# Sum of the values made once per head and added by VectorE, in the last two pairs of each later batch

## The chip, the cores and the metric

The kernel runs on one core of a Trainium2 chip. The metric is the device time of one execution in microseconds (us). TensorE does the matrix products and transposes into PSUM, VectorE, ScalarE and GpSimd work element by element, and SyncE mostly issues the transfers. VectorE and ScalarE read PSUM, and so each matmul's result has to be picked up by one of them.

## The reference

Attention over hash buckets, followed by a channel mix. B = 4 batches, H = 8 heads, S = 768 rows, D = 64.

```python
q_bucket = sum(((q @ proj) > 0) * 2**arange(6)); k_bucket likewise
scores = where(q_bucket[i] == k_bucket[j], q k^T / 8, -1e9)
attn = exp(scores - max); attn = attn / (attn.sum(-1) + 1e-9)
x = (attn @ v), heads side by side           # [B, S, 512]
xk, xr = mixes of x and x shifted by one row with mu_k, mu_r
out = sigmoid(xr @ w_r) * (max(xk @ w_k, 0)**2 @ w_v)
```

A row of q whose bucket no key shares gets the mean of all rows of v: all its scores are equal. The kernel must give that too.

## The kernel before, in words

Two heads make a pair n; there are 16 pairs, 0 to 15, four to a batch (`NPB` = 4). A head's keys are cut into six blocks of 128 (`NC_` = 6). The main loop has 192 slots, G = 12 n + s: slot s of pair n does head j = s // 6, key block jc = s % 6. In each slot `score` makes the block's scores for all 768 queries (L487, two matmuls of 384 columns), and ScalarE takes the exponential (L494) into a tile `pt`. Two slots later (`LAG` = 2) `pv` multiplies it with the values: six matmuls L515, one per query block, 65 columns each (64 of v and a column of ones, which gives the row's sum), all accumulated in one PSUM bank `oo` of 128x390 floats. Between these, in an order that is written out by hand and fixed when the program is made, stand the matmuls of the channel mix of the batch before (`ffn`, L584: `kp`, `rp`, `vp`), the preparation of pair n + 2 (`prepare`: VectorE's stream transposes L384, GpSimd's casts L389, the hash bits L446 with their signs L399), and the outputs of pair n - 1 (`turn_out` in slot 3).

The mean of the values enters as a very small weight on every key, EPS = 2^-60. GpSimd's `values` sums v over the six key blocks into `vs` (128x65). In `pv`, at a head's first block, one matmul L506 with the constant matrix `epsm` (128x128, all EPS) and `vs` repeated six times writes EPS times the sum of all values into the six query blocks of `oo`; the L515 matmuls add to it.

At a head's last block VectorE takes the reciprocal of the row sums (`rc`, L526) and writes the scaled head to `ob` (L527). The first head ends in slot 7 of its pair, the second in slot 1 of the next. In slot 3 of the next pair `turn_out` turns `ob` with six transposes L544 into a bank `ot`, VectorE copies it into `xt` (L545, L549), and the mix of x and its shifted rows follows on VectorE (L555, L569, L572). Behind L527 in VectorE's queue there can also stand `os` (L642, the product that ends an output block of the channel mix) and `k` (L621, a square).

Four PSUM banks serve `oo`, `ot`, the bits and the channel mix. `take` gives the one that has been free longest, and `give` puts it back once its last reader has been issued; the next writer waits for that reader. The scores have two buffers of two banks each of their own.

Of the kernel before, what the change touches and what calls it, by code (L numbers as in the profile page):

```python
# [9 lines left out]
FP32 = mybir.dt.float32  # L10
BF16 = mybir.dt.bfloat16
INT32 = mybir.dt.int32
AF = mybir.ActivationFunctionType
ALU = mybir.AluOpType
AX = mybir.AxisListType

P = 128
# [7 lines left out]
EPS = 2.0 ** -60  # L25
# [11 lines left out]
def kernel(  # L37
# [13 lines left out]
    nc = tc.nc  # L51
    B, H, S, D = q.shape
# [3 lines left out]
    NC_ = S // P  # L56
    HALF = S // 2
    NDC = DM // P
    NFC = DF // P
    NPB = H // 2  # L60
    NPAIRS = B * NPB
    NTE = 4
# [7 lines left out]
    epsm = consts.tile([P, P], BF16, name="epsm")  # L70
# [97 lines left out]
    def fast():  # L168
        with ExitStack() as fx:
            pool = lambda nm, bufs, **kw: fx.enter_context(  # L170
                tc.tile_pool(name=nm, bufs=bufs, **kw)
            )
# [7 lines left out]
            ptp = pool("pt", 6)  # L180
            obp = pool("ob", 2)
            rcp = pool("rc", 4)
            xtp = pool("xt", 2)
            aug = pool("aug", 1)
            dfp = pool("df", 2)
# [11 lines left out]
            def take(shape, dt, name):  # L197
                which = idle_banks.pop(0)
                return which, bkp.tile(shape, dt, name=name, tag=f"bk{which}")

            def give(which):
                idle_banks.append(which)
# [3 lines left out]
            NSET = 3  # L206
# [4 lines left out]
            augs, vas, vss = [], [], []  # L211
# [16 lines left out]
            nats, blks, vfs, pts, obs, xts, t32s, oos, held = ({} for _ in range(9))  # L228
# [251 lines left out]
            def score(n, j, jc):  # L480
# [18 lines left out]
                    scale=SCALE / 2.0 if (n, j) == TWICE else SCALE,  # L499
                )  # L500

            def pv(n, j, jc):
                if jc == 0:
                    taken, oos[n, j] = take([P, NC_, D + 1], FP32, f"oo{n}_{j}")
                    held[n, j] = taken
                    nc.tensor.matmul(  # L506
                        oos[n, j],
                        epsm,
                        vss[n % NSET][j][:, None, :].to_broadcast([P, NC_, D + 1]),
                        start=True,  # L510
                        stop=False,
                    )
                oo = oos[n, j]
                for ic in range(NC_):
                    nc.tensor.matmul(  # L515
                        oo[:, ic, :],
                        pts[n, j, jc][:, ic * P : (ic + 1) * P],
                        vas[n % NSET][j][:, jc, :],
                        start=False,
                        stop=(jc == NC_ - 1 and ic == NC_ - 1),  # L520
                    )
                if jc == NC_ - 1:
                    if j == 0:
                        obs[n] = obp.tile([P, NC_, P], BF16, name=f"ob{n}", tag="ob")
                    rc = rcp.tile([P, NC_], FP32, name=f"rc{n}_{j}", tag="rc")
                    nc.vector.reciprocal(rc, oo[:, :, D])  # L526
                    nc.vector.scalar_tensor_tensor(  # L527
                        out=obs[n][:, :, j * D : (j + 1) * D],
                        in0=oo[:, :, 0:D],
                        scalar=ROOT_HALF,  # L530
                        in1=rc.to_broadcast([P, NC_, D]),
                        op0=ALU.mult,
                        op1=ALU.mult,
                    )
                    give(held.pop((n, j)))

            def turn_out(n):
                b, t = divmod(n, NPB)
                xt = xtp.tile([P, P + S], BF16, name=f"xt{n}", tag="xt")
                held[n], ot = take([P, S], BF16, f"ot{n}")  # L540

                for i in range(NC_):
                    c = 2 * (i % 3) + i // 3 if n < NTE else i
                    nc.tensor.transpose(ot[:, c * P : (c + 1) * P], obs[n][:, i, :], ident16)  # L544
                nc.vector.tensor_copy(xt[:, P : P + S], ot)  # L545
                xts[b, t] = xt, ot

                nc.vector.memset(xt[:, 0:1], 0.0)
                nc.vector.tensor_copy(xt[:, 1:P], ot[:, S - P : S - 1])  # L549


            mx = {}
# [337 lines left out]
            def outputs(n, s):  # L890
                if n < 1:
                    return
                if s == 3:
                    turn_out(n - 1)
                if s == 4:
                    pieces.extend(mix((n - 1) // NPB, (n - 1) % NPB))
                if pieces and s >= 4:
                    pieces.pop(0)()
# [58 lines left out]
            for G in range(nslots + LAG):  # L957
                clock[0] = G
                n, s = divmod(G, 12)
# [13 lines left out]
                if old and not first:  # L973
                    pv(*old)
# [11 lines left out]
                if old and first:  # L986
                    pv(*old)
# [12 lines left out]
            ffn(2 * rate)  # L1000
            step()
            turn_out(NPAIRS - 1)
            for x, op in enumerate(mix(B - 1, NPB - 1)):
                if x < 3:
# [194 lines left out]
    with tc.manual_schedule():  # L1199
        fast()  # L1200
# [33 lines left out]
```

## Time and profile before

| | |
|---|---|
| median of three runs | 250.59 us (250.33 to 250.74) |
| profiled execution, its own time | 250.4 us |
| its span, first to last instruction | 248.5 us |
| TensorE busy | 240.3 us, 97% of the span |
| ScalarE busy | 208.6 us, 84% |
| VectorE busy | 167.7 us, 67% |
| GpSimd busy | 113.5 us, 46% |
| granted TensorE clock, mean | 0.996 |

The profile is of one execution. PE is TensorE, PEld its weight loads (they overlap the matmuls), DVE VectorE, ACT ScalarE, POOL GpSimd; SPq, ACTq are queues that issue transfers. L12 is line 12 of the kernel before. A group's row gives the tiles written and read, the partitions and elements, how often, the busy time, and the mean duration. The "idle before" of a row is time in which its engine stood still ahead of it, with what ended the wait. A few per cent of the matmul records are missing from the trace, which shows as a step that is one matmul too long. Some of the numbers are steps from one start to the next or the distance from one instruction's end to another's start, read from the timeline.

### The profile page before, as it was taken

The page shows a single profiled execution, that of the slowest core. Times are in us where ns is not written, and L with a number is a line of the kernel's source. Part 1 is how long each engine was busy: PE and PEld are TensorE (multiplying, and loading weights), DVE is VectorE, ACT ScalarE, POOL GpSimd, SP SyncE. Part 2 cuts the span into 40 slices and gives each one's busy share as a digit, 9 for nine tenths or more (in the row PEclk, how much of TensorE's full clock was granted, in tenths as well). Part 3 has the DMA queues.
Part 4 walks back from the last instruction along what each step waited for, and adds up shares of the span by engine and source line. Part 5 has one row for each costly group of instructions (what it writes and reads, how often), then busy time and mean ns, then how long its engine had stood idle before and what let it go on. Part 6 is the DMA issues. An engine that isn't in the chain of part 4 may idle for free.

```text
span 248.5 us, 6652 instructions
## 1 busy us (share of the span) xinstructions
PE 240.3 (97%) x2422; PEld 145.9 (59%) x2444; DVE 167.7 (67%) x389; ACT 208.6 (84%) x344; POOL 113.5 (46%) x214
## 2 busy tenths in 40 slices
PE   7999999999999999999999999999999999999993
PEld 4576666565656655565656556565666565555442
DVE  2887887887887738575787838476696627399421
ACT  4899999999999979789999979789999999639510
POOL 5989877697546370815537280815528000000000
PEclk9999999999999999999999999999999999999998
DMA  6989879396999384948729485955920111120132
GB/s 203 377 188 241 191 181 201 111 184 172 193 218 198 111 208 120 257 87 223 164 78 226 113 187 148 254 123 164 181 69 6 49 42 45 48 79 3 48 125 92
DMA packets 28231, 36.71 MB, mean 148 GB/s; under 512 B 3216, under 2 KB 25376, under 8 KB 28192
## 3 DMA queue, kind: packets, MB, share of 16 engines
q1 hardware_dynamic: 25744, 33.21, 50.9%
q0 software_dynamic: 2160, 2.62, 6.8%
q8 instruction: 21, 0.34, 0.7%
q10 hardware_dynamic: 288, 0.39, 0.5%
q14 instruction: 18, 0.15, 0.2%
HBM read 31.99 MB, written 6.29 MB: 154 GB/s over the span
## 4 chain that ended last, share of the span: by engine, by line
PE 85%; ACT 8%; DMA 4%; issue 1%; SPq 1%; DVE 0%; ACTq 0%
PE sc L487 23%; PE vp L584 16%; PE kp L584 16%; PE oo L515 12%; PE rp L584 8%; ACT pt L494 7%; PE bb L446 3%; DMA qk<-in_q_dram 2%; PE tp L327 2%; PE oo L506 2%; PE ot L544 2%; DMA aq<-sg 2%; PE bb L419 1%; ACT kr L615 0%; ACT sq L310 0%
## 5 line engine op out<-in xcount | busy, mean ns | idle before, releaser
L494 ACT ACTIVATE pt<-sc 128x768 bf16<-128x768 f32 x192 | 151.2, 814 | 16.3 <-PE sc L487 13.6
L487 PE MATMUL sc<-aq,ak 70*128 70x384 bf16 (+1 forms) x384 | 93.8, 325 | 1.4 <-ACT pt L494 0.5
L515 PEld LDWEIGHTS <-pt 128*128 128x128 bf16 x1152 | 60.6, 97 | 26.4
L515 PE MATMUL oo<-va,pt 128*128 128x65 bf16 x1152 | 66.3, 193 | 0.0
L584 PE MATMUL kp<-xk,wk_sb 128*128 128x384 bf16 x256 | 52.8, 326 | 0.2 <-ACT kr L615 0.2
L584 PE MATMUL vp<-wv_sb,k 128*128 128x512 bf16 (+1 forms) x184 | 50.4, 369 | 0.6
L487 PEld LDWEIGHTS <-ak 70*128 70x128 bf16 (+1 forms) x384 | 34.3, 97 | 26.9 <-issue 4.6
L389 POOL TENSOR_SCALAR aq<-t 64x768 bf16<-64x768 f32 x24 | 19.9, 828 | 61.1 <-DVE t L384 39.8
L621 DVE TENSOR_TENSOR k<-kr 128x384 bf16<-128x384 bf16 x64 | 28.5, 455 | 11.7 <-ACT kr L615 11.2
L642 DVE SCALAR_TENSOR_TENSOR os<-th,vp 128x512 f32<-128x512 bf16 (+1 forms) x25 | 16.6, 663 | 19.5 <-PE vp L584 13.0
L584 PEld LDWEIGHTS <-wk_sb 128*128 128x128 bf16 x256 | 21.6, 97 | 13.6 <-issue 3.8
L615 ACT ACTIVATE kr<-kp 128x384 bf16<-128x384 f32 x50 | 25.0, 499 | 4.4 <-PE kp L584 4.4
L584 PE MATMUL rp<-wr_sb,xr 128*128 128x512 bf16 x90 | 26.8, 379 | 0.3
L584 PEld LDWEIGHTS <-k 128*128 128x128 bf16 x200 | 16.8, 97 | 10.8 <-issue 1.3
L632 ACT ACTIVATE th<-rp 128x512 bf16<-128x512 f32 x24 | 14.2, 593 | 10.0 <-PE rp L584 8.0
L389 POOL TENSOR_SCALAR ak<-t 64x768 bf16<-64x768 f32 x24 | 20.2, 840 | 5.0 <-DVE t L384 1.7
L384 DVE STREAM_TRANSPOSE t<-bl 128x768 f32<-128x768 f32 x24 | 22.3, 956 | 0.0
L545 DVE COPY xt<-ot 128x768 bf16<-128x768 bf16 x16 | 8.9, 558 | 19.3 <-PE ot L544 19.3
L310 ACT ACTIVATE sq<-bl 128x768 bf16<-128x768 f32 x24 | 20.2, 841 | 0.0
L475 POOL TENSOR_TENSOR s<-vf 128x192 f32<-128x192 f32 x32 | 19.9, 622 | 0.0
L527 DVE SCALAR_TENSOR_TENSOR ob<-oo,rc 128x384 bf16<-128x384 f32 x32 | 17.8, 557 | 1.1
L473 POOL CAST va<-vf 128x384 bf16<-128x384 f32 x32 | 16.9, 527 | 3.3 <-DMA vf<-in_v_dram 2.5
(76 smaller groups left out, 220.1 us busy)
## 6 DMA issues: line engine op xcount, KB each, us to landing
bl<-in_q_dram SPq DMA_DIRECT2D x48, 176.0 KB
bl<-in_k_dram SPq DMA_DIRECT2D x48, 176.0 KB
vf<-in_v_dram SPq DMA_DIRECT2D x15, 384.0 KB
out_dram<-os SPq DMA_DIRECT2D x18, 256.0 KB
out_dram<-os SPq DMA_DIRECT2D x12, 128.0 KB
qk<-in_q_dram SPq DMA_DIRECT2D x3, 384.0 KB
qk<-in_k_dram SPq DMA_DIRECT2D x3, 384.0 KB
wk_sb<-in_moe_w_k_dram POOLq DMA_DIRECT2D x2, 512.0 KB, 6.8
```

Source lines behind the costliest of these rows:

```text
L310: nc.scalar.activation(junk, src, AF.Square, accum_out=acc)
L384: nc.vector.transpose(t32(n)[:, i].rearrange("p h (c f x) -> p (h c) f x", c=3, f=4), src)
L389: eng.tensor_scalar(out=augs[n % NSET]["qk"[i], j][ROWS[j], :], in0=t32(n)[ROWS[j], i].rearrange("p h y -> p (h y)"), scalar1=(1.0, ALPHA)[i],
L473: nc.gpsimd.tensor_copy(to, of)
L475: nc.gpsimd.tensor_add(s3, vf[:, 0 : 3 * D], vf[:, 3 * D : 6 * D])
L487: nc.tensor.matmul(sc[:, sp, 0:HALF], au["k", j][kr, jc * P : (jc + 1) * P], au["q", j][kr, sp * HALF : (sp + 1) * HALF], start=True, stop ...
L494: nc.scalar.activation(pt.rearrange("p (s q) -> p s q", s=2), sc[:, :, 0:HALF], AF.Exp, bias=EXP_BIAS, scale=SCALE / 2.0 if (n, j) == TWIC ...
L515: nc.tensor.matmul(oo[:, ic, :], pts[n, j, jc][:, ic * P : (ic + 1) * P], vas[n % NSET][j][:, jc, :], start=False, stop=(jc == NC_ - 1 and ...
L527: nc.vector.scalar_tensor_tensor(out=obs[n][:, :, j * D : (j + 1) * D], in0=oo[:, :, 0:D], scalar=ROOT_HALF, in1=rc.to_broadcast([P, NC_, D]),
L584: nc.tensor.matmul(box["t"], lhs(), rhs(), start=(i == 0), stop=(i == len(mms) - 1))
L615: nc.scalar.activation(kr, kp, AF.Relu)
L621: 1, lambda: nc.vector.tensor_tensor(out=k2, in0=kr, in1=kr, op=ALU.mult)
```

## The change

In pairs 6, 7, 10, 11, 14 and 15 (`late`: the last two pairs of batches 1, 2 and 3) the L506 matmul at a head's start is left out, and the head's first L515 matmul opens the accumulation. Instead, in `turn_out` of the pair before, two matmuls with `epsm` make EPS times the sum of all values once for each head, 64 columns each, in the part of the bank `ot` that the transposes leave free (768 bf16 columns are 384 floats, and 128 of the bank's 512 remain). VectorE copies them to two constant tiles `vb`, whose 65th column GpSimd sets once at the start. At such a head's end VectorE adds `vb`, repeated six times, to `oo` and writes the sum to a tile `su` in SBUF. The reciprocal and the scaled write read `su`, and the bank of `oo` is given back after the add.

```diff
+            vbs = [sup.tile([P, D + 1], FP32, name=f"vb{j}") for j in range(2)]
+            for vb in vbs:
+                nc.gpsimd.memset(vb[:, D : D + 1], float(NC_ * P) * EPS)
+
+            def late(n):
+                return n >= NTE and n % NPB in (2, 3)
...
             def pv(n, j, jc):
                 if jc == 0:
...
-                    nc.tensor.matmul(
-                        oos[n, j],
-                        epsm,
-                        vss[n % NSET][j][:, None, :].to_broadcast([P, NC_, D + 1]),
-                        start=True,
-                        stop=False,
-                    )
+                    if not late(n):
+                        nc.tensor.matmul(
...
-                        start=False,
+                        start=(late(n) and jc == 0 and ic == 0),
                         stop=(jc == NC_ - 1 and ic == NC_ - 1),
                     )
                 if jc == NC_ - 1:
...
+                    if late(n):
+                        su = sup.tile([P, NC_, D + 1], FP32, name=f"su{n}_{j}", tag="su")
+                        nc.vector.tensor_tensor(
+                            su, oo, vbs[j][:, None, :].to_broadcast([P, NC_, D + 1]), op=ALU.add
+                        )
+                        give(held.pop((n, j)))
+                        oo = su
                     rc = rcp.tile([P, NC_], FP32, name=f"rc{n}_{j}", tag="rc")
                     nc.vector.reciprocal(rc, oo[:, :, D])
...
-                    give(held.pop((n, j)))
+                    if not late(n):
+                        give(held.pop((n, j)))

             def turn_out(n):
...
-                held[n], ot = take([P, S], BF16, f"ot{n}")
-
+                held[n], bank = take([P, 512], FP32, f"ot{n}")
+                ot = bank[:, 0:HALF].bitcast(BF16)
+                if n + 1 < NPAIRS and late(n + 1):
+                    for j in range(2):
+                        nc.tensor.matmul(
+                            bank[:, HALF + j * D : HALF + (j + 1) * D],
+                            epsm,
+                            vss[(n + 1) % NSET][j][:, 0:D],
+                            start=True,
+                            stop=True,
+                        )
                 for i in range(NC_):
...
                 nc.vector.tensor_copy(xt[:, 1:P], ot[:, S - P : S - 1])
+                if n + 1 < NPAIRS and late(n + 1):
+                    for j in range(2):
+                        nc.vector.tensor_copy(
+                            vbs[j][:, 0:D], bank[:, HALF + j * D : HALF + (j + 1) * D]
+                        )
```

`sup` is a new SBUF pool with one buffer per tile. The bank that each `take` returns, and the order of all other instructions on each engine, are the same in both programs.

More of the change, by code (lines that the diff above doesn't have):

```diff
@@ L182, in fast @@
             rcp = pool("rc", 4)
+            sup = pool("su", 1)
             xtp = pool("xt", 2)
@@ L505, in pv @@
                     held[n, j] = taken
-                    nc.tensor.matmul(
-                        oos[n, j],
-                        epsm,
-                        vss[n % NSET][j][:, None, :].to_broadcast([P, NC_, D + 1]),
-                        start=True,
-                        stop=False,
-                    )
+                    if not late(n):
+                        nc.tensor.matmul(
+                            oos[n, j],
+                            epsm,
+                            vss[n % NSET][j][:, None, :].to_broadcast([P, NC_, D + 1]),
+                            start=True,
+                            stop=False,
+                        )
                 oo = oos[n, j]
@@ L539, in turn_out @@
                 xt = xtp.tile([P, P + S], BF16, name=f"xt{n}", tag="xt")
-                held[n], ot = take([P, S], BF16, f"ot{n}")
+                held[n], bank = take([P, 512], FP32, f"ot{n}")
[4 more added lines that the diff above has]
+                            bank[:, HALF + j * D : HALF + (j + 1) * D],
+                            epsm,
+                            vss[(n + 1) % NSET][j][:, 0:D],
+                            start=True,
+                            stop=True,
+                        )
                 for i in range(NC_):
@@ L549, in turn_out @@
                 nc.vector.tensor_copy(xt[:, 1:P], ot[:, S - P : S - 1])
+                if n + 1 < NPAIRS and late(n + 1):
+                    for j in range(2):
+                        nc.vector.tensor_copy(
+                            vbs[j][:, 0:D], bank[:, HALF + j * D : HALF + (j + 1) * D]
+                        )
             mx = {}
```

## The prediction

> **What bounds the kernel now.** I read the page first (busy shares, the 40 slices, the chain that ended last), because they say which engine's time is the kernel's time.
>
> ```profile
> PE 240.3 (97%) x2422; PEld 145.9 (59%) x2444; DVE 167.7 (67%) x389; ACT 208.6 (84%) x344; POOL 113.5 (46%) x214
> PE   7999999999999999999999999999999999999993
> PE 85%; ACT 8%; DMA 4%; issue 1%; SPq 1%; DVE 0%; ACTq 0%
> ```
>
> TensorE is busy in every slice after the first, and 85% of the chain is its work; VectorE, which is to get the new work, has no share of the chain. A busy share can hide stalls, so next come the waits between 74 and 216 us, the stretch that holds pairs 6 to 15 and so every place that the change touches.
>
> ```profile
> DVE xt L545 <- PE ot L544: 14.8, 10, 2.3
> ...
> DVE rc L526 <- PE oo L515: 10.2, 6, 3.6
> ...
> PEld L584 <- issue: 5.0, 8, 0.6
> ...
> PE sc L487 <- issue: 0.2, 1, 0.2
> ```
>
> The columns are total us, times, and the longest. VectorE waits for TensorE (25.0 us in these two rows); no row has TensorE waiting for VectorE. The gaps of up to 0.6 us are weight loads, which run ahead of the matmuls: at 102.23 a load stands 0.62 us after the one before it, while the eight fp32 matmuls L446 are still at work. The table of stages says how much room the others have there.
>
> ```profile
> 130.70:159.10 28.40, 28.14 (x284) 16.39 (x287) 18.42 (x39) 25.26 (x41) 14.56 (x26) 1.00 0.73 182
> ...
> 187.30:216.20 28.90, 28.63 (x287) 17.40 (x291) 15.49 (x36) 25.39 (x41) 4.61 (x10) 1.00 0.11 40
> ```
>
> After the stretch and its length come PE, PEld, DVE, ACT, POOL, then the granted clock (1.00). In pairs 10 and 11 (first line) TensorE is busy for 28.14 of 28.40 us, VectorE for 18.42: 10 us of VectorE are free per two pairs. In pairs 14 and 15 it is 13.4 us. ScalarE is the next fullest, with some 3 us free. So TensorE's instruction stream is the time here, and what is taken out of it comes back one to one as long as nothing it needs arrives later.
>
> **What is taken out.** The change touches heads of pairs 6, 7, 10, 11, 14 and 15, so 12 heads. Each loses one L506 matmul of 390 columns. Its cost is not its duration (331 ns) but the step from its start to the next start, since matmuls overlap:
>
> ```profile
> 140.23 0.38 PE L584 MATMUL vp<-wv_sb,k 128*128 128x512 bf16 x1
> 140.44 0.33 PE L506 MATMUL oo<-vs,epsm 128*128 128x390 bf16 x1
> 140.61 0.34 PE L515 MATMUL oo<-va,pt 128*128 128x65 bf16 x6
> 140.79 0.49 PE L487 MATMUL sc<-aq,ak 128*128 128x384 bf16 x2
> ```
>
> L506 starts at 140.44 and the next matmul at 140.61: 0.17 us. The same step stands at the other late heads I read. 12 x 0.17 = 2.04 us removed. The wait for a free bank and for `vs` moves from L506 to the first L515; there is no time in it, since no such wait shows now.
>
> **What is added on TensorE.** Two matmuls of 64 columns with a weight load each, ahead of the transposes of `turn_out`, in six pairs: 12 in all. The nearest row is L515, 65 columns with a load each: six of them take the step from 140.61 to 140.79, 0.030 us each. 12 x 0.030 = 0.36 us. The far bound is that none of them overlaps: an L515 matmul's whole duration, 193 ns, 12 x 0.193 = 2.3 us, which would eat the gain. I take 0.030, because these loads use the same stream and the loads of L515 stay hidden in it 1152 times. The Trainium skill (TensorE: Matmul & The Clock Gate, Back-to-back issue gap) speaks against the change here: it gives about 81 ns per matmul in a stream of weight loads and 128-column matmuls. By it the 12 would be 0.97 us, and the net gain on TensorE 1.07 instead of 1.68. The trace does not agree with it: the six 128-column transposes L544 with a load each take 0.50 us, the last lasting 0.219, so 56 ns apart.
>
> Net on TensorE: 2.04 - 0.36 = 1.68 us.
>
> **What is added on VectorE.** Per head an add of 128x390 floats from PSUM. The row nearest is L527, the scaled write of 128x384 from PSUM, 557 ns; L642 with 512 columns takes 684, so 1.0 ns per column and 563 for 390. A dependent VectorE instruction starts 0.03 to 0.04 us after the one before it ends (`rc` to `ob`), so the chain at a head's end grows by 0.60 us. `rc` and `ob` then read SBUF. Bounds for `ob`: 398 ns (L345, 384 floats SBUF to SBUF, one tensor) and today's 557; I take 557. Per pair two copies of 64 columns from PSUM: about 0.22 us each (L549, 127 bf16 columns from PSUM, takes 220; by L527 less 320 columns it is 237). Sum: 12 x (0.60 + 0.22) = 9.8 us over six pairs, 1.6 us a pair, against the 5 to 6.7 us free per pair. It does not make VectorE the bound; what counts is where it is late.
>
> One thing is not in that sum. `ob` now has both inputs in SBUF, and such instructions stretch when GpSimd works:
>
> ```profile
> L527 DVE SCALAR_TENSOR_TENSOR ob<-oo,rc x32: 556/557/558, 15.8 to 215.3; 128x384 bf16<-128x384 f32 x32
> L621 DVE TENSOR_TENSOR k<-kr x64: 346/358/1006, 55.4 to 229.4; 128x384 bf16<-128x384 bf16 x64
> ```
>
> The numbers are minimum, median, maximum. L527, one input in PSUM, never varies, though it too runs beside GpSimd. L621, both inputs in SBUF, goes from 346 to 1006 ns, and the long ones lie beside GpSimd work, as the 864 ns at 130.35. So `ob` can lose up to 0.65 us at the second heads of pairs 6, 7, 10 and 11, where GpSimd prepares `values` at that time (0.3 to 0.6 us per instruction); at first heads GpSimd is idle until the stream transposes that follow, and in pairs 14 and 15 it has almost nothing left. The Trainium skill (SBUF — State Buffer, SBUF: two separate sides) says the same of a VectorE instruction with two SBUF inputs against a GpSimd one that reads SBUF: one blocks for the whole of the other. The trace agrees, with the 1006 against 346.
>
> **Who waits for that.** (a) The transposes L544 need `ob`. Pair 10's second head: `ob` ends at 147.58 and the weight load for its transposes starts at 148.87, 1.29 us later; for 6, 7, 11 and 14 the distance is 1.51, 1.28, 1.29, 1.28. TensorE gets there up to 0.11 sooner where the next head also loses its L506. 0.60 is covered, 0.60 + 0.5 just so. (b) Pair 15's has no such cover:
>
> ```profile
> 215.11 0.20 DVE L526 RECIPROCAL rc<-oo 128x6 f32<-128x6 f32 x1 [3.64 <-PE oo L515]
> 215.34 0.56 DVE L527 SCALAR_TENSOR_TENSOR ob<-oo,rc 128x384 bf16<-128x384 f32 x1
> ...
> 216.21 0.54 PEld L544 LDWEIGHTS <-ob 128*128 128x128 bf16 x6
> ```
>
> `ob` ends at 215.90, the load starts at 216.21. With the add, `ob` ends at 215.11 + 0.56 + 0.04 + 0.19 + 0.04 + 0.56 = 216.50, plus 0.04 to be seen: TensorE stands still for 0.33 us (0.15 if `ob` takes 398). (c) Banks that VectorE frees: behind the add in its queue is `os` L642, which frees the bank of a `vp`; I paired each bank's release with its next first write in the timeline, and the nearest cases that stand behind an added instruction are 0.92 to 1.24 us apart (vp's bank freed at 151.32, written again at 152.24). The copies (0.44) or the add (0.60) use part of it. (d) The stream transposes L384 behind the first head's add feed the bits L446: 0.55 us of cover in pair 7 (100.90 to 101.45), 1.3 to 2.0 in 6, 10 and 11. In pair 7 VectorE idles 0.44 before `os` at 94.02 and 0.59 before `os` at 99.32, waiting for TensorE; the copies and the add fall into these. Nothing lost. (e) ScalarE in pairs 14 and 15 runs without a gap for some stretches (from 193.84 to 204.1), and the scores there follow the exponential that frees their buffer by 0.12 us at the least. I take 0.05 us lost. (f) GpSimd's two one-column memsets at the start (0.1 us) stand before the first cast, whose result is needed half a microsecond later.
>
> Sum: 1.68 - 0.33 - 0.05 = 1.30 us less. The profiled execution took 250.4 (span 248.5 and 1.9 around it) and would take 249.1; the median of the runs is 250.59, 0.19 above it, so 249.3.
>
> **Rivals.** *The gain is mostly eaten on TensorE or by ScalarE* (0.14): a 64-column matmul is too short to hide the load behind it, so that the 12 cost 0.056 each, as the transposes do, instead of 0.03 (0.3 us more), and ScalarE, with 3 us free per two pairs, holds the scores back by 0.05 in each of the six late pairs (0.3 more): 249.9. For it speaks the 0.12 us of (e), against it the even steps of L515. The 81 ns that the Trainium skill gives (TensorE: Matmul & The Clock Gate, Back-to-back issue gap) would give the same: 1.07 - 0.38 = 0.69 less, 249.9. *VectorE's chain becomes what TensorE waits for, and it ends slower* (0.12): the six second heads have about 1.17 to 1.4 us of cover after the sooner arrival. An add of a form not seen in this trace (a float operand broadcast over six blocks) could take 1.0 us instead of 0.56; with 0.65 lost to GpSimd the delay is 1.69, so 0.52 us of standstill at four heads, none in pair 14, and 0.77 in pair 15: 2.85 lost against 1.68, time 251.8. It decides from a delay of about 1.45 us on. Against it: L527, also with a broadcast second input, takes 557 each time. *The change does nothing of the kind* is out: in the built programs' lists of instructions the 12 matmuls are gone and the 12 short ones are there, with the rest of TensorE's order kept.
>
> **How the numbers follow.** The forecast has 0.74; its own range is 248.9 (no tail loss) to 249.7. Some 0.2%, 0.5 us, is what a measurement can tell from no change. Faster by more: 0.74 and half of the first rival, 0.81; within: 0.07; slower: 0.12. The range for 8 in 10 runs from 248.8 to 250.2, which takes in the first rival and the bounds of the short matmuls up to about 0.1 each.
>
> **What would show it.** L506 count 20, not 32; steps of 0.03 at the 64-column matmuls; the add at about 560 ns; `ob` at 557 and longer in pairs 7, 8, 11 and 12 at their starts; a TensorE gap of 0.2 to 0.35 us before the last six transposes and no new wait of TensorE for VectorE elsewhere. The prediction is wrong if such waits stand before L544 in several pairs, or if the pairs with late heads don't shorten by 0.28 us each.

## The result and the profile after

The changed kernel takes 249.88 us (median of 19 runs, 248.74 to 250.75), the kernel before 250.80 in 19 runs made beside them. The ratio is 0.9949, 95% interval 0.9932 to 0.9967: 0.5% faster, 1.3 us of 250.8 (0.8 to 1.7). The two medians alone are 0.92 us apart. Forecast were 1.30 us less and a time of 249.3.

The page after, answering to the three lines shown of before. Line numbers are those of the kernel that a profile is of: the scores, L487 before, are L488 after.

```profile
PE 240.4 (97%) x2444; PEld 145.7 (59%) x2444; DVE 177.2 (71%) x413; ACT 208.4 (84%) x344; POOL 114.7 (46%) x216
...
PE   8899999999999999999999999999999999999992
...
PE 85%; ACT 7%; DMA 4%; issue 1%; SPq 1%; DVE 0%; ACTq 0%
```

VectorE has 9.5 us more to do (167.7 to 177.2) and still no share of the chain. TensorE's busy sum is no smaller, and that says little: a union of recorded spans depends on which records are missing (22 more matmul records here, of the same number of instructions).

The profiled execution took 250.22 us with a span of 248.1, only 0.4 less than before's 248.5, because the first scores start 0.69 us later (8.76 against 8.07) and the last write ends 0.34 us longer after the last `os`. Both belong to transfers. The transposes ahead of the first scores, in TensorE's timeline, before and then after (start, us, what, and in brackets the idle time ahead):

```profile
7.71 0.52 PE L327 MATMUL tp<-ident,qk 128*128 128x128 f32 x3 [0.19 <-DMA qk<-in_q_dram]
```

```profile
8.41 0.52 PE L328 MATMUL tp<-ident,qk 128*128 128x128 f32 x3 [0.88 <-DMA qk<-in_q_dram]
```

They wait for a piece of q to land, which came 0.7 us later in this execution. So I compare a **stretch**: from the first score matmul to the end of the last `os`. It is 236.82 us before and 235.34 after, 1.48 less. The distances between the first scores of neighbouring pairs split it (us, from the timelines; the last column is from pair 15's first score to the last `os`):

| | 5 | 6 | 7 | 8 | 9 | 10 | 11 | 12 | 13 | 14 | 15 and tail |
|---|---|---|---|---|---|---|---|---|---|---|---|
| before | 14.16 | 14.20 | 14.14 | 14.10 | 14.17 | 14.20 | 14.14 | 14.10 | 14.17 | 13.31 | 44.23 |
| after | 14.16 | 13.93 | 13.87 | 14.10 | 14.17 | 13.93 | 13.87 | 14.10 | 14.17 | 13.04 | 44.11 |

Each pair with late heads is 0.27 shorter, the others are the same to 0.01, and pair 15 gives back part of its 0.27. From pair 5 to the last `os` it is 184.93 before and 183.44 after, 1.49 less. The step where L506 (now L516) stood, in the timeline of TensorE:

```profile
134.94 0.22 PE L563 MATMUL ot<-vs,epsm 128*128 128x64 bf16 x2
134.99 0.50 PE L572 MATMUL ot<-ident,ob 128*128 128x128 bf16 x6
...
140.28 0.38 PE L617 MATMUL vp<-wv_sb,k 128*128 128x512 bf16 x1
140.49 0.34 PE L525 MATMUL oo<-va,pt 128*128 128x65 bf16 x6
140.67 0.49 PE L488 MATMUL sc<-aq,ak 128*128 128x384 bf16 x2
```

`oo` follows the `vp` matmul by 0.21, as L506 did before; the 0.17 is gone. The two short ones take 0.055 together. The waits between 74 and 216 us:

```profile
DVE su L538 <- PE oo L525: 10.0, 6, 3.5
DVE xt L573 <- PE ot L572: 9.6, 10, 1.3
...
PEld L617 <- issue: 5.6, 9, 0.6
...
PEld L572 <- DVE ob L545: 0.5, 1, 0.5
PEld L525 <- ACT pt L495: 0.2, 1, 0.2
```

VectorE's wait for the transposes fell from 14.8 to 9.6: the longer chains at the second heads used that idle time. TensorE waits for VectorE once. VectorE's new groups:

```profile
L545 DVE SCALAR_TENSOR_TENSOR ob<-su,rc 128x384 bf16<-128x384 f32 x12 | 7.7, 644 | 0.4
...
L538 DVE TENSOR_TENSOR su<-oo,vb 128x390 f32<-128x390 f32 x12 | 6.7, 562 | 10.0 <-PE oo L525 10.0
...
L580 DVE COPY vb<-ot 128x64 f32<-128x64 f32 x12 | 2.1, 215 | 0.0
```

The add takes 562 ns, a copy 215, `ob` from `su` 644 on average.

### The profile page after: what moved, and what is told of

Its sections match the earlier page's. It is cut to its first block, busy times and chain, and to the rows that moved or that the text cites. A ratio compares the mean times of both kernels' runs of the same rounds, so it can differ in the third digit from the quotient of the medians.

```text
span 248.1 us, 6709 instructions
## 1 busy us (share of the span) xinstructions
PE 240.4 (97%) x2444; PEld 145.7 (59%) x2444; DVE 177.2 (71%) x413; ACT 208.4 (84%) x344; POOL 114.7 (46%) x216
## 4 chain that ended last, share of the span: by engine, by line
PE 85%; ACT 7%; DMA 4%; issue 1%; SPq 1%; DVE 0%; ACTq 0%
PE sc L488 23%; PE vp L617 17%; PE kp L617 16%; PE oo L525 12%; PE rp L617 8%; ACT pt L495 6%; PE bb L447 3%; DMA qk<-in_q_dram 2%; PE tp L328 2%; PE ot L572 2%; DMA aq<-sg 2%; PE bb L420 1%; PE oo L516 1%; ACT sq L311 0%; SPq L253 0%
## 5 line engine op out<-in xcount | busy, mean ns | idle before, releaser
L488 PE MATMUL sc<-aq,ak 70*128 70x384 bf16 (+1 forms) x384 | 93.8, 325 | 1.1 <-ACT pt L495 0.5
L617 PE MATMUL vp<-wv_sb,k 128*128 128x512 bf16 (+1 forms) x200 | 54.4, 370 | 0.0
L488 PEld LDWEIGHTS <-ak 70*128 70x128 bf16 (+1 forms) x384 | 34.4, 98 | 26.9 <-issue 4.6
L654 DVE TENSOR_TENSOR k<-kr 128x384 bf16<-128x384 bf16 x64 | 29.1, 465 | 11.6 <-ACT kr L648 11.2
L617 PE MATMUL rp<-wr_sb,xr 128*128 128x512 bf16 x96 | 27.7, 379 | 0.0
L476 POOL TENSOR_TENSOR s<-vf 128x192 f32<-128x192 f32 x32 | 21.2, 664 | 0.0
L538 DVE TENSOR_TENSOR su<-oo,vb 128x390 f32<-128x390 f32 x12 | 6.7, 562 | 10.0 <-PE oo L525 10.0
```

What stands on the lines that cost most here:

```text
L476: nc.gpsimd.tensor_add(s3, vf[:, 0 : 3 * D], vf[:, 3 * D : 6 * D])
L488: nc.tensor.matmul(sc[:, sp, 0:HALF], au["k", j][kr, jc * P : (jc + 1) * P], au["q", j][kr, sp * HALF : (sp + 1) * HALF], start=True, stop ...
L617: nc.tensor.matmul(box["t"], lhs(), rhs(), start=(i == 0), stop=(i == len(mms) - 1))
L654: 1, lambda: nc.vector.tensor_tensor(out=k2, in0=kr, in1=kr, op=ALU.mult)
```

## The experiments

The pair distances of one profile, and with them the stretch, carry most verdicts, because the runs' times scatter by a few tenths of a per cent. In the profiles the pairs from 5 on repeat to 0.01 us where the program is the same; the early ones do not (pairs 0 and 1 together took 20.75 to 21.50 over all runs), so a stretch can be off by some 0.7, and the verdicts are read from the pairs.

**What L506 costs.** The kernel before, with L506 twice at the 12 heads:

```diff
+                    for x in range(2 if n >= NTE and n % NPB in (2, 3) else 1):
-                    nc.tensor.matmul(
+                        nc.tensor.matmul(
                             oos[n, j], epsm, vss[...],
                             start=True,
-                            stop=False,
+                            stop=(x == 0 and n >= NTE and n % NPB in (2, 3)),
                         )
```

> The kernel before, with L506 issued twice at the 12 late heads. Theory (one L506 costs its step, 0.17 us, not its duration, 0.331): 12 x 0.17 = 2.04 us more than before, stretch 238.85. Rival (its duration counts): 4.0 us more; rival (it lies beside other work): no change.

Pairs 6, 7, 10, 11 and 14 became 14.54, 14.48, 14.54, 14.48 and 13.65 long: 0.34 each, 0.17 per matmul, and the last piece 0.35. That is 2.05 in all; the stretch (239.18) is 2.36 longer, and the rest lies in pairs 0 and 1. Time 253.18 against 251.05, ratio 1.0092 (1.0061 to 1.0123). The step is the price.

**What the short matmuls cost.** Four times each:

```diff
-                    for j in range(2):
+                    for j in (0, 1) * 4:
                         nc.tensor.matmul(
                             bank[:, HALF + j * D : HALF + (j + 1) * D], epsm, ...
```

> The changed kernel with the two 64-column matmuls in turn_out made four times each: 36 more. Theory (0.028 us each, as their step in the trace of the changed kernel): 1.0 us more, stretch 236.35. Rival (some 0.08 us each, load and matmul together): 2.9 us more, stretch 238.2. The step in the trace, and the stretch, tell which.

```profile
134.84 0.40 PE L563 MATMUL ot<-vs,epsm 128*128 128x64 bf16 x8
135.07 0.50 PE L572 MATMUL ot<-ident,ob 128*128 128x128 bf16 x6
```

Eight take 0.23: 0.029 each. The pairs are 0.17 to 0.18 longer than in the changed kernel (14.10, 14.04, 14.11, 14.05, 13.21), 0.028 to 0.03 for each of the six more; the stretch is 236.29. The Trainium skill (TensorE: Matmul & The Clock Gate, Back-to-back issue gap) gives about 81 ns per load and matmul of 128 columns; neither these (29 ns) nor the 128-column transposes (56 ns apart) come to it, and the measurement decides. Time 250.65 against 251.13, ratio 0.9975 (0.9938 to 1.0012).

**Whether VectorE's work counts.** The add made twice:

```diff
                     if late(n):
...
+                        for _ in range(2):
-                        nc.vector.tensor_tensor(
+                            nc.vector.tensor_tensor(
```

> The changed kernel with the add at each of the 12 late heads made twice: 12 x 0.60 = 7.2 us more for VectorE, TensorE's stream the same. Theory (VectorE's work costs only where it outruns the cover before the transposes): ob ended 0.42 to 0.77 us ahead of the load in pairs 6, 7, 10, 11 and 14, so the doubled add uses up the cover and loses at most 0.2 in each; pair 15 loses 0.6 more; together 0.6 to 1.5, stretch 235.9 to 236.8. Rival (VectorE's busy time counts as such): 7.2 us more, stretch 242.

The stretch is 236.59, 1.25 more, and pairs 5 to 15 give 1.19 of it, where VectorE got 12 x 0.60 = 7.2 us more. The waits between 74 and 218 us name the largest part:

```profile
PEld L573 <- DVE ob L546: 1.1, 1, 1.1
...
PE ot L573 <- DVE ob L546: 0.6, 1, 0.6
```

That is pair 15 (44.71 instead of 44.11). Pairs 7 and 11 are 0.15 and 0.17 longer, because the bits now stand before VectorE's stream transposes are through (these end at 101.67, the first of the eight matmuls went out at 101.57), and pairs 8 and 12 0.13 each. The sum fell into the expected range, but I had put the loss at the transposes, and of these only pair 15's lost more than 0.02. Pair 8 shows the place instead:

```profile
106.63 0.67 DVE L676 SCALAR_TENSOR_TENSOR os<-th,vp 128x512 f32<-128x512 bf16 x1
...
106.76 0.45 PEld L573 LDWEIGHTS <-ob 128*128 128x128 bf16 x6
...
106.89 0.50 PE L573 MATMUL ot<-ident,ob 128*128 128x128 bf16 x6
```

The transposes wait for nothing to speak of, but the `vp` matmul behind them starts at 107.36, 0.19 after the last of them (0.06 in the changed kernel): its bank is freed by the `os` that ends at 107.30, behind `ob` in VectorE's queue. Pairs 6, 10 and 14 lost nothing. Time 250.92 against 251.05, ratio 0.999 (0.9953 to 1.0027).

**Why `ob` stretches.** The sum written back to PSUM:

```diff
-                        su = sup.tile([P, NC_, D + 1], FP32, name=f"su{n}_{j}", tag="su")
...
-                            su, oo, vbs[j][:, None, :].to_broadcast([P, NC_, D + 1]), op=ALU.add
+                            oo, oo, vbs[j][:, None, :].to_broadcast([P, NC_, D + 1]), op=ALU.add
                         )
-                        give(held.pop((n, j)))
-                        oo = su
...
-                    if not late(n):
-                        give(held.pop((n, j)))
+                    give(held.pop((n, j)))
```

> The changed kernel, but the add writes its sum back into the PSUM bank, so that the reciprocal and the scaled write ob read PSUM again (one input of ob in SBUF instead of two); the bank is given back after ob. Theory (ob took 707 to 916 ns at the second heads of pairs 6, 7, 10, 11 because of two inputs in SBUF beside GpSimd's work): ob is 557 at all 12 heads, and ends 0.7 to 0.9 us ahead of the load there instead of 0.42 to 0.62; the time stays, since that was covered: stretch 235.3. Rival (it was VectorE's queue or the rows of su): the long ob stay.

The instructions that write or read `ob`, in the changed kernel and then here (minimum, median, maximum):

```profile
L545 DVE SCALAR_TENSOR_TENSOR ob<-oo,rc x20: 557/557/559, 16.5 to 189.6; 128x384 bf16<-128x384 f32 x20
L545 DVE SCALAR_TENSOR_TENSOR ob<-su,rc x12: 557/557/916, 84.2 to 215.0; 128x384 bf16<-128x384 f32 x12
```

```profile
L542 DVE SCALAR_TENSOR_TENSOR ob<-oo,rc x32: 557/558/559, 16.2 to 214.8; 128x384 bf16<-128x384 f32 x32
```

The long ones are gone, with the same queue and the same neighbours on GpSimd. `ob` ends 0.97, 0.68, 0.75 and 0.68 ahead of the weight load in pairs 6, 7, 10 and 11 (0.62, 0.42, 0.62, 0.42 in the changed kernel). The pairs have the changed kernel's lengths: it was covered. What the Trainium skill says of two SBUF inputs beside GpSimd (SBUF — State Buffer, SBUF: two separate sides) fits: taking one of them away ends the stretching. The stretch, 235.65, is longer by what pairs 0 and 1 took. Time 249.72 against 251.13, ratio 0.9967 (0.9933 to 1.0001).

**The standstill at pair 15.** Two more `vp` matmuls ahead of the last transposes:

```diff
-            ffn(2 * rate)
+            ffn(2 * rate + 0.4)
             step()
             turn_out(NPAIRS - 1)
```

> The changed kernel, but two more matmuls of the channel mix (0.43 us) stand ahead of the transposes of pair 15, as cover for the longer chain of VectorE at that head's end; nothing else moves. Measure: from the start of the first score matmul to the end of the last os, 236.81 us before and 235.34 in the changed kernel (first landing and last write lie outside it). Theory (the stall of 0.13 us of TensorE before these transposes is the only one that the change made): the gap is gone and the stretch is 235.2; the time falls against the changed kernel by 0.13. Rival (the later start of the mixing chain of pair 15 is paid again at the first kp group): the gap turns up 20 matmuls later, stretch 235.3 or longer.

The standstill of 0.13 before the transposes is gone, and the stretch is 235.31, the changed kernel's: the rival was right, somewhat earlier than it said. The timeline of the two engines shows the first mix of pair 15 ending later relative to TensorE:

```profile
216.98 3.25 PE L617 MATMUL kp<-xk,wk_sb 128*128 128x384 bf16 x18
...
217.43 0.42 DVE L602 TENSOR_SCALAR xk<-df,mu_sb 128x768 bf16<-128x768 bf16 x1
...
217.89 0.56 DVE L605 TENSOR_TENSOR xk<-xk,xt 128x768 bf16<-128x768 bf16 x1
218.37 0.68 DVE L675 SCALAR_TENSOR_TENSOR os<-th,vp 128x512 f32<-128x512 bf16 x1
```

`xk` ends at 218.45 and the `kp` matmul that needs it starts at 218.50, 0.06 late; another 0.11 is lost at 219.10, where a bank is wanted that the `os` behind `xk` frees at 219.05. The tail is bound by VectorE's chain from the add over `ob`, `xt` and `xk` to this `os`. Time 249.45 against 251.05, ratio 0.9936 (0.9912 to 0.9959), not to be told from the changed kernel's.

**How far the change carries.** All pairs from 5 on:

```diff
             def late(n):
-                return n >= NTE and n % NPB in (2, 3)
+                return n > NTE
```

> The changed kernel with the rule widened from the last two pairs of each later batch to all pairs from 5 on: 5, 8, 9, 12 and 13 lose their L506 too. Theory (TensorE's stream is the time and each pair gives 0.27 us): 5 x 0.27 = 1.35 us less than the changed kernel, stretch 234.0. Rival (VectorE, with the squares of the channel mix in pairs 8, 9, 12 and 13, is late there: banks that it frees have only 0.1 to 0.4 us of cover, and ob stretches beside GpSimd): TensorE stands still for 0.1 to 0.6 us in each of these four pairs, and the stretch is 234.6 to 236.

Pairs 8 and 12 became 13.83, 0.27 shorter, as TensorE's sum has it. Pairs 5 and 9 became 14.34 and 14.35, 0.18 longer, and 13 gained nothing (14.19); the stretch is 235.46. The waits between 60 and 216 us have a row that was in no run before, and the timeline shows its place in pair 9:

```profile
PEld bb L447 <- DVE t L385: 0.8, 3, 0.3
```

```profile
129.00 1.83 DVE L385 STREAM_TRANSPOSE t<-bl 128x768 f32<-128x768 f32 x2
...
130.43 0.14 PEld L447 LDWEIGHTS bb<-t,projp 128*32 128x32 f32 x2 [0.18 <-issue]
130.43 1.30 PE L447 MATMUL bb<-t,projp 128*32 128x384 f32 x8
...
130.89 0.15 PEld L447 LDWEIGHTS bb<-t,projp 128*32 128x32 f32 x6 [0.32 <-DVE t L385]
```

The stream transposes end at 130.83; the bits have begun at 130.43 and take 1.30 instead of 0.85. In pairs 5, 9 and 13 the cover of the bits was 0.55 to 0.70 before, and add and copies are more. Neither banks nor `ob` cost anything. So both theories were half right: VectorE is late in these pairs, but at one place; that the squares make it so was not tried. Time 249.69 against 251.05, ratio 0.9961 (0.9937 to 0.9985).

**Two ways out.** First, the wide version with the bits one slot later:

```diff
+                if s == 0 and 6 <= n + 1 < NPAIRS:
+                    bits_dve(n + 1)
                 m = n + 2
...
-                if s == 11:
-                    bits_dve(m)
```

> The run with all pairs from 5 on late, but the bits of a pair stand one slot later in TensorE's order (slot 0 of the next pair, some 1.1 us later), nothing else moved. Theory (pairs 5, 9 and 13 lost 0.46 us because the bits stood in the queue before the stream transposes were through): the wait of the bits for L385 is gone, pairs 5, 9 and 13 come down to about 13.9, stretch 234.0. Rival (it was VectorE's backlog as such, or the signs and their transfer then come too late for the scores): the loss turns up at another wait, stretch 235 or more.

The wait is gone, pairs 5, 9 and 13 are 14.04, 14.03 and 14.03, but pairs 8 and 12 rose to 14.03 too, and the stretch is 235.66. The rival was right in kind, not in place. The move also puts bits into pair 14 (13.92 instead of 13.04) and takes as many out of pair 4, which gains less (12.15 instead of 12.52). With no bits between a pair's last scores and the next pair's first, the scores reach ScalarE's exponential early: in pairs 6, 9, 10, 13 and 14 they start 0.05 us after the exponential that frees their buffer (0.7 and more in the changed kernel), the smallest distance seen anywhere, and TensorE stands still for 0.14 to 0.21 there. In pair 9:

```profile
115.18 0.81 ACT L495 ACTIVATE pt<-sc 128x768 bf16<-128x768 f32 x1
...
115.35 0.65 PE L617 MATMUL kp<-xk,wk_sb 128*128 128x384 bf16 x3
...
116.04 0.48 PE L488 MATMUL sc<-aq,ak 70*128 70x384 bf16 x2
```

The last of the three `kp` starts at 115.68, and the scores 0.36 later instead of 0.17. Time 249.59 against 251.09, ratio 0.9948 (0.9919 to 0.9976).

Second, leave pairs 5, 9 and 13 as they were:

```diff
             def late(n):
-                return n >= NTE and n % NPB in (2, 3)
+                return n > NTE and n % NPB != 1
```

> The changed kernel with the rule widened to pairs 8 and 12 (late: 6, 7, 8, 10, 11, 12, 14, 15), pairs 5, 9 and 13 left as before. Theory (in the run with all pairs from 5 on, 8 and 12 were 0.27 us shorter, and 5, 9 and 13 lost their gain because the bits waited for VectorE's stream transposes): 0.54 us less than the changed kernel, stretch 234.8, pairs 8 and 12 at 13.83, pairs 9 and 13 at 14.17, no wait of the bits. Rival (the delay in pairs 9 and 13 comes from the pair before them, whose second head ends there): pairs 9 and 13 stay longer than 14.17.

Pairs 8 and 12 are 13.83, 9 and 13 are 14.17, no wait of the bits; the stretch is 234.91. Time 249.22 against 251.09, ratio 0.9916 (0.9883 to 0.9950). By its pairs it beats both kernels, the changed one by 0.54 us; the intervals of the two ratios overlap.

**The changed kernel again**, on the chip of the two runs just told:

> The changed kernel once more, on the same chip as the two others: stretch 235.3, time 0.5% below the kernel before; a second profile shows how far the start (first score at 8.76 us) and the end belong to the change. Theory (they are scatter of the first landing and the last write): other values here with the same pair lengths. Rival (the two memsets on GpSimd delay the start): the first score again 0.7 us later than before.

Time 249.87 against 251.09, ratio 0.9975 (0.9944 to 1.0006); by these runs alone it could not be told from no change. The first score starts at 8.47, pair 0 takes 11.50, and pairs 5 to 15 have the same lengths to 0.01 (183.44 again). The start is mostly scatter: the first score comes at 8.07 and 8.29 in the two profiles without the two memsets and at 8.21 to 9.49 in those with them. The memsets move GpSimd's first cast from 6.24 to 6.46 us, and a delay of a tenth or two by them is not excluded; pair 0 took 10.74 both without them and, in the first profile, with them. The stretch (235.99) missed its 235.3 by pairs 0 and 1.

## Why the prediction was right, point by point

- *TensorE's stream is the time.* Shown: what left it came back one to one (0.27 per late pair), and what was put in cost its full step (0.34 and 0.17 per pair), while 7.2 us more on VectorE cost 1.19.
- *Removed: 12 x 0.17 = 2.04.* The doubled L506 gave 0.17 each.
- *Added: 12 x 0.030 = 0.36.* Compared start by start in the two traces, the transposes behind the short matmuls lose 0.053 to 0.062 per pair, 0.35 in all; the far bound (0.193) and the rival's 0.056 each were not met. The net of 0.28 per pair came out as 0.27.
- *Add 563, chain longer by 0.60, copies 0.22, `ob` 557 plus up to 0.65.* Measured: 562; in pair 10 the add starts at 146.68 and the reciprocal at 147.28, 0.60 apart; 215; and `ob` 0.15 to 0.36 over 557 at the four heads named. The PSUM version shows that `su` in SBUF, as the second such input, is the cause.
- *Who waits.* (a) held with 0.42 to 0.77 of cover left. (c) and (d) held, with 0.50 of cover for the bits in pairs 7 and 11 (0.55 and 1.26 before). They are the places that give way first once VectorE gets more, as the doubled add and the wide version show.
- *Pair 15's standstill, 0.33.* This is the term that was too large: TensorE stood still for 0.13, under the 0.2 to 0.35 named as a sign. (Of the 0.15 given for an `ob` of 398 ns, the prediction's own sum makes 0.17.)

```profile
215.01 0.56 DVE L545 SCALAR_TENSOR_TENSOR ob<-su,rc 128x384 bf16<-128x384 f32 x1
...
215.28 0.38 PE L617 MATMUL vp<-wv_sb,k 128*128 128x512 bf16 x1
...
215.62 0.34 PEld L572 LDWEIGHTS <-ob 128*128 128x128 bf16 x6 [0.46 <-DVE ob L545]
215.63 0.51 PE L572 MATMUL ot<-ident,ob 128*128 128x128 bf16 x6
```

`ob` ended 0.05 before the load, and the load was 0.34 late, as worked out. But a load goes out one matmul ahead (before, load and `vp` matmul both start at 216.21, the transposes at 216.42): here it could have started at 215.28, together with the `vp` matmul, and that one filled the array for 0.21 of the 0.34. The distance to the load understates the cover by the matmul in front of it.
- *ScalarE, 0.05.* A load waited 0.2 for an exponential; no matmul was late by more than 0.02.

By these, 2.04 - 0.35 - 0.13 = 1.56 was to be had; pairs 5 to 15 gave 1.49, and no wait in the trace holds the rest. So the terms were right but for the tail, and the forecast of 1.30 was some 0.2 too small; that the ratio gives 1.3 is in part luck, since its interval (0.8 to 1.7) takes in 1.49 as well.

The median, 249.88, lies on the 249.9 of the first rival and not on the 249.3, but neither of that rival's terms was met: the short matmuls cost 0.029 each and ScalarE held back no scores, and so the pairs are 0.27 shorter, where its sum makes 0.18. The slower rival failed at its price, an add of 1.0 us; its mechanism, a late VectorE that TensorE waits for, is real and was met in the wide version.

## What to carry to other kernels

Price a matmul by the step to the next start, in the stream where it stands, and count an engine off the chain as free only up to the distance from its result to the first instruction that wants it. Look for that distance at each consumer and in each stage: here the same edit gave 0.27 us in pair 8 and cost 0.18 in pair 9, by one wait. When scatter at the ends of a run is as large as the effect, compare the distances between marks inside it.

## What the hardware showed that I had not expected

The stretching goes both ways: beside pair 10's `ob` a GpSimd add (L476) took 0.90 us, where that instruction takes 0.59 elsewhere in the same stretch. It is the same at the second heads of pairs 6, 7 and 11 (0.90 each), and at all four places the add takes 0.59 to 0.60 in the kernel before and in the PSUM version, where `ob` has one input in PSUM.

```profile
147.51 0.71 DVE L545 SCALAR_TENSOR_TENSOR ob<-su,rc 128x384 bf16<-128x384 f32 x1
...
147.76 0.90 POOL L476 TENSOR_TENSOR s<-vf 128x192 f32<-128x192 f32 x1
```
